# Four norm and head-group paths turned through DRAM instead of on TensorE, and a new list order, in a one-core attention and feed-forward kernel

## The chip, the cores and the metric

The kernel runs on one core of one Trainium2 chip. Times are microseconds (us) of device time of one execution. Before the change the median of three runs is 845.14 us (844.97 to 845.48). The engines are called by the names of the profile: PE is TensorE, PEld its weight loads, DVE is VectorE, ACT is ScalarE, POOL is GpSimd, SP is SyncE, which here issues the DMAs.

## The reference

A pre-norm block: attention over a dilated window of eight positions, then a SwiGLU feed-forward part, each with a residual. S = 2048 tokens, D = 640, 32 heads of 20, F = 1728.

```python
def _A_ref(x, wqkv, wo):
    qkv = (x @ wqkv).reshape(B, S, 3, H, Dh).transpose(2, 0, 3, 1, 4)
    q, k, v = qkv[0], qkv[1], qkv[2]
    idx = pos[:, None] - (jnp.arange(8) * 2)[None, :]
    ...
    logits = jnp.einsum("bhsd,bhswd->bhsw", q, kg) * Dh ** -0.5
    logits = jnp.where(mask[None, None, :, :], logits, -1e9)
    o = jnp.einsum("bhsw,bhswd->bhsd", softmax(logits), vg)
    return o.transpose(0, 2, 1, 3).reshape(B, S, D) @ wo
def _B_ref(x, w_gate, w_up, w_down):
    return (silu(x @ w_gate) * (x @ w_up)) @ w_down
h = x + _A_ref(layernorm(x), wqkv, wo)
out = h + _B_ref(layernorm(h), w_gate, w_up, w_down)
```

## The kernel before

**Blocks.** The 2048 tokens are four blocks of 512 (b = 0 to 3), each held as four rows of 128 partitions (j = 0 to 3). The heads are four groups of eight (g = 0 to 3, 160 columns each). Every fp32 product on PE is made of three passes over operands split into a high part (ACT's cast) and a low part (DVE's subtraction).

**Stages of a block.** (1) The first norm of x, and its transposition into columns, which PE needs as the stationary operand. (2) QKV (L546), group by group, 15 matmuls of 480 columns for each row; ACT evicts and scales (L551), and q, k and v go to the DRAM buffers qsc, ksc, vsc. (3) Attention, on DVE: it loads q, k and v windows, multiplies (L595), reduces (L602), takes maximum and difference (L613, L614); ACT makes the exponential; DVE sums and normalises (L624 to L626), multiplies by v (L630) and halves the products down (L638). The output is turned by 32 x 32 blocks (STREAM_TRANSPOSE, L668) and stored to the DRAM buffer osc, from where it comes back in columns. (4) The output projection, called wo(b): columns from osc are split (L783, or L711 in the blocks named in TURNED), and PE runs eight pieces of 15 matmuls of 320 columns (L793); the row of x is added (L799, L804). (5) The second norm of the sum, transposed into columns again. (6) The feed-forward part in 14 tiles of 128 columns: gate and up (L863), the gate on DVE (L898, L909), down (L874). For the last two blocks this stage works on pairs of column combinations, which save matmuls (L958, L980, their operands from column_combinations). (7) A transposition back (L1160) and the final addition.

**Three ways into columns.** On PE, four transposes of 128 x 128 into one PSUM bank, then a cast and a subtraction out of it (L507 for block 0's first norm, L439 in `to_columns`, L404 in `pair_columns`, L733 in `last_columns`). Through DRAM, a whole block: `turn_rows` turns 128 x 2560 on DVE by 32 x 32 blocks (L412) and stores it in four DMAs to ysc (L414), `turned_back` loads it (L420), and `turned_columns` casts and subtracts from SBUF (L428, L429). Through DRAM, the first half of a block: `turn_pair` (L381, buffer zsc) and `pair_columns` (L395, L396), which leaves PE ten transposes for the other half.

**Which block goes which way** is said by four tuples. TURN names blocks whose second norm goes through DRAM wholly, HALF those of which the first half does, TURN1 those whose first norm does. TURNED is the other way round: blocks whose last head group is transposed on PE (`last_columns`, L733) instead of going through osc.

**Order.** All operations are collected in a `Plan`, each with its engine, an assumed cost, its dependencies by memory ranges and a priority from the table PR. `order()` starts them greedily by priority, sorts by the start found plus an entry of SHIFT, and every engine then runs its operations in that fixed order. An operation that has to wait holds up everything behind it on its engine; SP's DMAs too are issued in this order.

**Weights.** QKV weights come in 20 pieces through a staging buffer of eight slots (L519); each is cast by ACT (L520) and split by DVE (L522). The output weights use the same staging (L685, split at L688), so their load waits until the pieces that lie there are split. Feed-forward weights are split in block 0 (L857), the low parts stored to lsc and loaded again later.

## Time and profile before

| what | us |
|---|---|
| median of three runs | 845.14 (844.97 to 845.48) |
| the profiled execution | 845.0 |
| its span, first to last instruction | 843.0 |
| ACT busy | 406.5 |
| DVE: L595, L602, L630, 32 each of about 2.8 us | 270.4 |
| DMA engines, share of the span | 65.7% |

The span is what the profile records; 2.0 us of the execution's time lie outside it. Matmuls are pipelined: the time given for one is from its start to its modelled end, while the next has started already, so what a matmul costs PE is the distance between starts. In the timeline, a row with a count (x10) is a run of equal operations, with the start of the first and the time until the end of the last. "DVE operation b <- ACT a" in the list of waits means that DVE stood idle until ACT ended a. The DMA lines give the median time from issue to landing. The granted TensorE clock was 1.0 throughout.

### The profile page before, as it was taken

How to read it: one execution, taken by the hardware profiler on the slowest of the kernel's cores; microseconds unless marked ns; L12 is line 12 of the kernel's file. 1: busy time of each engine (PE TensorE's matmuls, PEld its weight loads, DVE VectorE, ACT ScalarE, POOL GpSimd, SP SyncE). 2: the span in 40 equal slices, each digit the busy share in tenths (PEclk: the TensorE clock that was granted, in tenths of full speed). 3: DMA queues.
4: the chain of work that ended last, by engine and by line, in shares of the span. 5: the costliest groups of instructions: out<-in, count | busy, mean ns of one | idle time of the engine just before them, and what ended most of it. 6: DMA issues, size and time to landing. Idle time of an engine off the chain costs nothing.

```text
span 843.0 us, 10782 instructions
## 1 busy us (share of the span) xinstructions
PE 837.8 (99%) x3961; PEld 712.0 (84%) x3961; DVE 705.1 (84%) x841; ACT 406.5 (48%) x674; POOL 24.8 (3%) x33
## 2 busy tenths in 40 slices
PE   9999999999999999999999999999999999999998
PEld 7888888889888888888888898888888888888886
DVE  8899899999998999999999999899434996655552
ACT  6662462344663433775434467456447543333331
POOL 0000000000000100010000010000000000000000
PEclk9999999999999999999999999999999999999999
DMA  8886487467488779468987975888833554444432
GB/s 288 327 314 237 145 272 268 137 209 236 153 290 304 242 257 332 164 207 279 338 329 242 342 242 165 262 329 286 307 111 104 193 177 157 154 169 144 154 113 89
DMA packets 90260, 191.12 MB, mean 227 GB/s; under 512 B 31568, under 2 KB 50896, under 8 KB 89568
## 3 DMA queue, kind: packets, MB, share of 16 engines
q1 hardware_dynamic: 90208, 190.44, 65.7%
q8 instruction: 31, 0.51, 0.2%
q14 instruction: 21, 0.17, 0.1%
HBM read 144.26 MB, written 46.14 MB: 226 GB/s over the span
## 4 chain that ended last, share of the span: by engine, by line
PE 99%; ACT 0%; POOL 0%; DVE 0%; issue 0%; POOLq 0%
PE bank L546 25%; PE bank L874 22%; PE bank L863 22%; PE bank L958 18%; PE bank L793 8%; PE bank L980 2%; PE bank L439 1%; PE bank L454 1%; PE bank L507 0%; PE bank L404 0%; PE bank L1160 0%; PE bank L733 0%; ACT sha L509 0%; POOL ra L1194 0%; DVE h L1168 0%
## 5 line engine op out<-in xcount | busy, mean ns | idle before, releaser
L863 PE MATMUL bank<-shb,ra 128*128 128x512 f32 x810 | 190.2, 390 | 0.0
L863 PEld LDWEIGHTS bank<-shb,ra 128*128 128x128 f32 x810 | 151.4, 188 | 31.4 <-DVE shb L443 0.3
L874 PE MATMUL bank<-ra,acts 128*128 128x512 f32 (+1 forms) x662 | 162.8, 389 | 0.0
L874 PEld LDWEIGHTS bank<-ra,acts 128*128 128x128 f32 x662 | 122.5, 188 | 24.6
L546 PE MATMUL bank<-ra,sha 128*128 128x480 f32 x480 | 105.9, 380 | 0.3 <-ACT sha L509 0.3
L546 PE MATMUL bank<-ra,shb 128*128 128x480 f32 x470 | 102.8, 378 | 0.0
L546 PEld LDWEIGHTS bank<-ra,sha 128*128 128x128 f32 x480 | 89.6, 188 | 14.1 <-ACT sha L509 0.6
L546 PEld LDWEIGHTS bank<-ra,shb 128*128 128x128 f32 x470 | 88.0, 188 | 13.2
L630 DVE TENSOR_TENSOR fa<-fa 128x2560 f32<-128x2560 f32 x32 | 90.3, 2822 | 0.8
L595 DVE TENSOR_TENSOR fa<-fa 128x2560 f32<-128x2560 f32 x32 | 90.2, 2820 | 0.4
L602 DVE TENSOR_REDUCE fa<-fa 128x128 f32<-128x2560 f32 x32 | 89.9, 2810 | 0.5
L551 ACT ACTIVATE st<-bank,fa 128x480 f32<-128x480 f32 x64 | 42.2, 661 | 95.5 <-PE bank L546 87.0
L958 PE MATMUL bank<-shb,ra 128*128 128x512 f32 x360 | 88.0, 391 | 0.0
L958 PEld LDWEIGHTS bank<-shb,ra 128*128 128x128 f32 x360 | 67.1, 188 | 13.5
L638 DVE TENSOR_TENSOR fa<-fa 128x1280 f32<-128x1280 f32 (+2 forms) x68 | 75.9, 1115 | 1.5
L1096 DVE TENSOR_TENSOR fa<-bank,fa 128x512 f32<-128x512 f32 x60 | 41.0, 690 | 42.1 <-PE bank L958 41.1
L793 PE MATMUL bank<-ra 128*128 128x320 f32 x480 | 74.6, 309 | 0.0
L793 PEld LDWEIGHTS bank<-ra 128*128 128x128 f32 x480 | 72.3, 188 | 2.2 <-DVE ra L711 0.2
L958 PE MATMUL bank<-ra 128*128 128x512 f32 x288 | 68.4, 390 | 0.0
L958 PEld LDWEIGHTS bank<-ra 128*128 128x128 f32 x288 | 53.9, 188 | 11.7 <-ACT shb L1017 0.4
L840 ACT CAST ra<-fa 128x1280 fp32r<-128x1280 f32 (+1 forms) x38 | 45.9, 1207 | 28.2 <-PE bank L863 21.4
L908 ACT CAST acts<-fa 128x512 fp32r<-128x512 f32 x47 | 29.1, 620 | 50.7 <-DVE fa L898 25.5
(152 smaller groups left out, 843.7 us busy)
## 6 DMA issues: line engine op xcount, KB each, us to landing
fa<-in_ffn_dram SPq DMA_DIRECT2D x46, 960.0 KB, 6.6
ra<-lsc SPq DMA_DIRECT2D x45, 320.0 KB, 3.4
fa<-ksc SPq DMA_DIRECT2D x16, 880.0 KB, 5.6
fa<-vsc SPq DMA_DIRECT2D x16, 880.0 KB, 6.9
ra<-lsc SPq DMA_DIRECT2D x21, 640.0 KB, 5.3
lsc<-ra SPq DMA_DIRECT2D x13, 640.0 KB, 5.8
ksc<-st SPq DMA_DIRECT2D x16, 320.0 KB, 2.6
qsc<-st SPq DMA_DIRECT2D x16, 320.0 KB, 2.7
```

What stands on the lines that cost most here:

```text
L546: T.matmul(banks[bk][:, 0:480], l, r_(wq(g, w, c), 480), start=(p, c) == first_mm, stop=(p, c) == last_mm)
L551: P.add("ACT", act(480) + 0.06, lambda bk=bk, j=j: A.activation(stage_t()[:, so : so + 1920].rearrange("p (t j c) -> p t j c", t=3, j=NJ)[ ...
L595: P.add("DVE", dve(2560), lambda: V.tensor_tensor(f(PROD, 2560).rearrange("p (j w c) -> p j w c", j=2, w=W), window(ko, 2 * jp), f(qo + 32 ...
L602: P.add("DVE", dve(2560), lambda: V.tensor_reduce(f(lo + 128 * jp, 128), f(PROD, 2560).rearrange("p (n d) -> p n d", d=DH), axis=AX.X, op= ...
L630: V.tensor_tensor(f(PROD, 2560).rearrange("p (j w d) -> p j w d", j=2, d=DH), bass.AP(tensor=fa[:, vo : vo + 160].tensor, offset=fa[:, vo ...
L638: V.tensor_add(dst(v), v[:, :, 0:m, :], v[:, :, m : 2 * m, :])
L793: T.matmul(banks[bk][:, 0:320], l, r_(m, 320), start=p == 0 and c == 0, stop=p == 2 and c == NC - 1)
L840: P.add("ACT", act(n), lambda: A.copy(r_(gu, n), f(raw, n)), r=[rf(raw, n)], w=[rr(gu, n)], prio=PR["fh"])
L863: T.matmul(banks[bk], r_(gu + 1280 * w + wid * c + col, 128), x2(a, c), start=p == 0 and c == 0, stop=p == 2 and c == NC - 1)
L874: T.matmul(banks[bk][:, lo:hi], l, m, start=first and p == 0, stop=last and p == len(passes) - 1)
L958: T.matmul(banks[bk], r_(ws[w] + 256 * q, 128), x(a, c), start=start and p == n == q == 0, stop=stop and p == 2 and n == len(terms) - 1 an ...
L1096: dv(0, lambda: V.tensor_add(fb(h, dst), banks[bk], fb(h, src)), [pb(bk)] + fr(h, src), fr(h, dst))
```

## The change

**Sets.** TURN goes from () to (3,): block 3's second norm goes through DRAM wholly. TURNED goes from (0, 3) to (3,): block 0's last head group goes through osc. HALF gains block 0, TURN1 gains block 1; the latter's first norm takes its statistics on ACT instead of DVE. `column_combinations` now reads the result in the layout that the DRAM path leaves, in operations of 512 columns instead of 1024. PE had 136 transposes and has 78.

**Order.** `order()` no longer goes by PR alone: after a first list by priority it computes, from PE's list backwards, the latest start of each operation (`latest`), lists again by that (`listed`), and does so in seven rounds. On DVE an operation that reads the result of the one before it is put behind another. The assumed costs are adjusted, and SHIFT has 57 entries instead of 12.

```diff
-TURN = ()
-TURNED = (0, 3)
-HALF = (1, 2)
-TURN1 = (2, 3)
+TURN = (3,)
+TURNED = (3,)
+HALF = (0, 1, 2)
+TURN1 = (1, 2, 3)
...
+LANES, HOP = 8, 0.035
+LAP = {"PE": 0.0, "ACT": 0.1, "DVE": 0.08, "POOL": 0.0, "SP": 0.0}
+ROUNDS = ((1.0, 20, 1.5), (1.5, 10, 3.5), (1.1, 0, 1.5), (1.4, 20, 3.5), (1.3, 3, 2.5), (1.2, 3, 2.5), (1.3, 20, 5.0),)
...
 SHIFT = {
-    10: 0.9, 12: 2.5, 34: 4.5, 47: -27.4, 113: 0.8, 131: -5.8, 2096: 10.8, 2101: 6.1, 2156: 4.1, 2712: 6.9,
...
+    26: 0.6, 31: -47, 34: -25.1, 35: -4.3, 39: -16.4, 42: 1.8, 53: -0.6, 118: 0.9, 136: -103.6, 214: 10.2, 241:
...
     def order(self):
+        start = self.listed()
+        for stretch, serial, dma in ROUNDS:
+            start = self.listed(self.latest(start, stretch, dma), serial)
...
+    def latest(self, start, stretch, dma):
+
+        ops = self.ops
+        t, due = 5.0, {}
+        for n in sorted((n for n, o in enumerate(ops) if o[0] == "PE"), key=lambda n: start[n]):
+            due[n] = t
+            t += ops[n][1]
+        last = [0.0] * len(ops)
+        for n in reversed(range(len(ops))):
+            eng, cost, _, _, prio, _, nbytes = ops[n]
+            if eng == "SP":
+                cost += nbytes + dma
+            elif eng == "DVE" and prio == 20:
+                cost *= stretch
+            last[n] = min(min((last[m] - HOP for m in self.succ[n]), default=1e9) - cost, due.get(n, 1e9))
+        return last
...
+            if e == "DVE" and before is not None:
+                n = min(ready[e], key=lambda x: (x[0] + serial * (before in ops[x[1]][3]), x))[1]
...
             if b:
-                if b == 1:
-                    st.prio = PR["ln1d"]
-                    for j in range(NJ):
-                        st.one_dve(j)
-                else:
-                    for j in range(NJ):
-                        st.one(j)
+                for j in range(NJ):
+                    st.one(j)
                 st.prio = 2
                 st.rstd(0, NJ)
-                if b in TURN1:
-                    turn_rows(ysc, "Y", b, PR["tr"], PR["yst"])
-                    return
-                x_columns(
...
+                if b:
+                    turn_rows(ysc, "Y", b, *((PR["y1"],) * 2 if b == 1 else (PR["tr"], PR["yst"])))
                 return
...
-            if b in (1, 2) and b not in HALF:
+            if b not in HALF and (b in (1, 2) or b in TURN):
                 stats.rstd(0, NJ)
                 for j in range(NJ):
                     stats.apply(j)
+            if b in TURN:
+                turn_rows(ysc, "Y", b, PR["g1"], PR["g1"])
...
-            dv(0, lambda: V.tensor_add(tv(0), y(0), y(2)), yr)
+            dvs(0, lambda i: V.tensor_add(part(tv(0), i), y(i), y(2 + i)), yr)
...
             if b < 3:
                 x_columns(lambda u: (shb[:, 512 * u : 512 * u + 512], shb[:, 2560 + 512 * u : 3072 + 512 * u]), lambda u: (hi(u), lo(u)), prio)
                 return
+            if b in TURN:
+                turned_back(ysc, "Y", b, PR["g1"])
+                turned_columns(lambda: r_(X3, 5120), "ra", PR["g1"])
+                return
...
                 elif b == 1:
                     load_x(b)
                     ln1(b)
+                    turned_back(ysc, "Y", b, PR["y1"])
+                    turned_columns(*xt(b), PR["y1"])
```

In the changed file the lines have moved: L580 is QKV, L827 the pieces of wo, L899 gate and up, L910 down, L1016 the first use of block 3's columns; L629 the attention multiplication by q, L556 the split of a QKV weight piece, L719 the load of the output weights, L619 the load of a K or V window; L447 and L767 the transposes on PE for half blocks and for the last head group; L745 and L817 the splits of osc columns; L455 and L457 the turn through DRAM and its stores, L463 the load back, L471 and L472 cast and subtraction.

**How it moves the first loads.** SP's order in the first 40 us, before. L557 and L565 store k, v and q of the first group, L585 loads a K or V window, L581 q, L685 the output weights:

```order
L557 DMA ksc<-st 64x2x640
L565 DMA qsc<-st 128x640
L557 DMA vsc<-st 64x2x640
L468 DMA fa<-in_x_dram 128x1x2560
L585 DMA fa<-ksc 128x1x1760
L581 DMA fa<-qsc 128x320 x2
L585 DMA fa<-vsc 128x1x1760
L557 DMA ksc<-st 64x2x640
L565 DMA qsc<-st 128x640
L557 DMA vsc<-st 64x2x640
L685 DMA fa<-in_wo_dram 128x640 x5
```

The same place now (L591 and L599 store k, v and q):

```order
L591 DMA ksc<-st 64x2x640
L553 DMA fa<-in_wqkv_dram 128x480
L599 DMA qsc<-st 128x640
L591 DMA vsc<-st 64x2x640
L719 DMA fa<-in_wo_dram 128x640 x2
L619 DMA fa<-ksc 128x1x1760
L615 DMA fa<-qsc 128x320 x2
L619 DMA fa<-vsc 128x1x1760
L457 DMA ysc<-fa 32x20x128 x4
```

Two loads of the output weights have come ahead of the first K window, the load of block 2's x has gone behind it, and the four stores of block 1's turned rows follow.

**How it moves wo(0) on PE.** Before, from the first piece of wo(0) to the end of block 0's transposes for the second norm:

```order
L793 MATMUL bank_75<-ra 128x320 x15
L793 MATMUL bank_73<-ra 128x320 x15
L793 MATMUL bank_74<-ra 128x320 x15
L793 MATMUL bank_75<-ra 128x320 x15
L733 MATMUL bank_73<-fa 32x128
L733 MATMUL bank_73<-fa 128x128
...
L439 MATMUL bank_75<-fa 128x128 x4
L439 MATMUL bank_74<-fa 128x128 x4
L546 MATMUL bank_70<-ra,shb 128x480 x15
L439 MATMUL bank_73<-fa 128x128 x4
L439 MATMUL bank_75<-fa 128x128 x4
L439 MATMUL bank_74<-fa 128x128 x4
```

Now:

```order
L827 MATMUL bank_74<-ra 128x320 x15
L827 MATMUL bank_75<-ra 128x320 x15
L827 MATMUL bank_73<-ra 128x320 x15
L827 MATMUL bank_74<-ra 128x320 x15
L580 MATMUL bank_70<-ra,shb 128x480 x15
...
L447 MATMUL bank_74<-fa 128x128 x4
L447 MATMUL bank_75<-fa 128x128 x4
L447 MATMUL bank_73<-fa 128x128 x2
```

The transposes of the last head group between the halves of wo(0) are gone, and the second norm keeps ten of its twenty.

**Block 3's second norm on DVE.** Before, it had no turn there; now it stands among the gates (L934, L945) of the feed-forward part, and ends in five subtractions, with the first of the column combinations (L1060, L1065) around them:

```order
L409 TENSOR_TENSOR fa<-fa 128x4
L934 TENSOR_TENSOR fa<-bank_74,fa 128x512
L945 TENSOR_TENSOR acts<-fa,acts 128x512
L455 STREAM_TRANSPOSE fa<-fa 128x2560
L934 TENSOR_TENSOR fa<-bank_74,fa 128x512
L945 TENSOR_TENSOR acts<-fa,acts 128x512
L934 TENSOR_TENSOR fa<-bank_74,fa 128x512
L945 TENSOR_TENSOR acts<-fa,acts 128x512
L1060 TENSOR_TENSOR fa<-fa 128x4x128
L1065 TENSOR_TENSOR fa<-shb,fa 128x4x128
L472 TENSOR_TENSOR ra<-fa,ra 128x4x128 x5
```

The turn (L455) and the five subtractions (L472) are what replaces the twenty transposes on PE of block 3.

More of the change, by code (lines that the diff above doesn't have):

```diff
@@ L68, in order, with listed @@
     def order(self):
+        start = self.listed()
+        for stretch, serial, dma in ROUNDS:
+            start = self.listed(self.latest(start, stretch, dma), serial)
+        self.start, self.end = start, max(t + o[1] for t, o in zip(start, self.ops))
         ops = self.ops
         left = [len(o[3]) for o in ops]
[L71 to L74 removed]
+        key = [(t + SHIFT.get(n, 0.0), n) for n, t in enumerate(start)]
+        heap, out = [key[n] for n in range(len(ops)) if not left[n]], []
+        heapq.heapify(heap)
+        while heap:
+            n = heapq.heappop(heap)[1]
+            out.append(n)
+            for m in self.succ[n]:
+                left[m] -= 1
+                if not left[m]:
+                    heapq.heappush(heap, key[m])
+        return out
+    def latest(self, start, stretch, dma):
[13 more added lines that the diff above has]
+        return last
+    def listed(self, last=None, serial=0.0):
+        ops = self.ops
+        left = [len(o[3]) for o in ops]
+        if last is None:
+            self.succ = [[] for _ in ops]
+            for n, o in enumerate(ops):
+                for d in o[3]:
+                    self.succ[d].append(n)
+        succ = self.succ
         avail = [0.0] * len(ops)
@@ L1013, in dv, with dvs @@
                 P.add("DVE", dve(size(n)), fn, r=r, w=tr(n), prio=PR["jp"])
+            def dvs(n, fn, r):
+                for i in range(size(n) // 512):
+                    P.add("DVE", dve(512), lambda i=i: fn(i), r=r, w=tr(n), prio=PR["jp"])
             def put(n, dst, key):
```

114 lines of the change are left out of this document (52 added, 62 removed), and 5 rows, old and new, of the table SHIFT.

## The prediction

> **What bounds the kernel now.** I read the page first: busy time, slices, the chain that ended last.
>
> ```profile
> span 843.0 us, 10782 instructions
> PE 837.8 (99%) x3961; PEld 712.0 (84%) x3961; DVE 705.1 (84%) x841; ACT 406.5 (48%) x674; POOL 24.8 (3%) x33
> DVE  8899899999998999999999999899434996655552
> PE 99%; ACT 0%; POOL 0%; DVE 0%; issue 0%; POOLq 0%
> ```
>
> TensorE (PE) is busy 837.8 of 843.0 us and is 99% of the chain: what leaves PE's list shortens the kernel, unless PE must then wait. The digits of VectorE (DVE) are the second fact: 9 in nearly every slice (21 us each) until about 600 us, looser behind that. So I asked next what PE waits for.
>
> ```profile
> PE bank L454 <- POOL ra L1194: 1.3, 1, 1.3
> PE bank L546 <- ACT sha L509: 0.3, 1, 0.3
> ```
>
> Those 1.6 us, both at the start, are all of its waits. But DVE keeps up only just. Here are the starts of the output projections wo(0) and wo(1) on PE (L793), with the DVE operation that each needs (L711, L783):
>
> ```profile
> 190.55 1.62 PE L793 MATMUL bank<-ra 128*128 128x320 f32 x10
> 190.37 0.42 DVE L711 TENSOR_TENSOR ra<-bank,ra 32x256 fp32r<-32x256 f32 x1
> 327.96 2.21 PE L793 MATMUL bank<-ra 128*128 128x320 f32 x14
> 326.13 1.03 DVE L783 TENSOR_TENSOR ra<-fa,ra 128x512 fp32r<-128x512 f32 x2
> 481.89 1.33 PE L793 MATMUL bank<-ra 128*128 128x320 f32 x8
> ```
>
> At wo(0) DVE ends (190.79) no earlier than PE's start, at wo(1) 0.8 us ahead of it (327.16). So the question is not only what the removed transposes cost, but whether DVE can follow a PE that comes earlier.
>
> **Term 1: the transposes leave PE.** The groups of them that the change touches, before:
>
> ```profile
> L439 PE MATMUL bank<-fa 128*128 128x128 f32 x60 | 8.0, 272 | 0.0
> L404 PE MATMUL bank<-fa 128*128 128x128 f32 x20 | 3.2, 272 | 0.0
> L733 PE MATMUL bank<-fa 128*128 128x128 f32 x8 | 2.0, 272 | 0.0
> L733 PE MATMUL bank<-fa 128*32 128x128 f32 x8 | 2.0, 272 | 0.0
> ```
>
> That is 96 (40 more, in block 0's first norm and in the last step, stay); the order of the changed kernel has 38 of them (30 at L447, 8 at L767): 58 fewer. The 272 ns are from start to modelled end and overlap with neighbours; what one costs PE is the distance between starts:
>
> ```profile
> 373.15 0.62 PE L863 MATMUL bank<-shb,ra 128*128 128x512 f32 x2
> 373.60 0.85 PE L874 MATMUL bank<-acts,ra 128*128 128x512 f32 x3
> 374.29 0.60 PE L404 MATMUL bank<-fa 128*128 128x128 f32 x4
> 374.64 1.64 PE L874 MATMUL bank<-ra,acts 128*128 128x512 f32 x6
> 29.13 1.47 PE L439 MATMUL bank<-fa 128*128 128x128 f32 x12
> 30.36 1.32 PE L546 MATMUL bank<-ra,sha 128*128 128x480 f32 x5
> ```
>
> Four take 374.64 - 374.29 = 0.35 us. The six matmuls behind them take 1.64; at 0.23 from start to start (0.69 for the three at 373.60) and 0.39 for the last I expect 5 x 0.23 + 0.39 = 1.54, so 0.10 more belongs to the four: 0.45, or 0.112 each. Twelve in a row take 1.23, 0.1025 each. The bounds are 0.0875 (0.35 / 4) and 0.112; 58 of them give 5.1 to 6.5 us. I take 0.11, since most were groups of four or less among other matmuls: **-6.4 us**. The number of other matmuls, and their sizes, are unchanged.
>
> The Trainium skill ("TensorE: Matmul & The Clock Gate", Part 4: PE-mode transpose) gives about 275 ns for a transpose within a kernel; the trace agrees as to duration (272). Taken as PE's cost it would make 58 x 0.275 = 16 us, an estimate by that page; the starts above speak against it.
>
> **Term 2: DVE's list against PE's.** DVE gains work: two more 2560-wide STREAM_TRANSPOSEs, one of 1280 and two of 320. It loses work as well: block 1's first norm takes its statistics on ScalarE (ACT), wo(0) needs fewer splits of turned pieces (20 before at L711, 10 after at L745; six more at L817), and the new order puts fewer operations directly behind the one that they read (191 such neighbours before, 127 after). The last is worth something:
>
> ```profile
> 165.89 2.83 DVE L595 TENSOR_TENSOR fa<-fa 128x2560 f32<-128x2560 f32 x1
> 168.75 2.82 DVE L602 TENSOR_REDUCE fa<-fa 128x128 f32<-128x2560 f32 x1
> 171.48 0.82 DVE L688 TENSOR_TENSOR ra<-fa,ra 128x640 fp32r<-128x640 f32 x1
> L412 DVE STREAM_TRANSPOSE fa<-fa 128x2560 f32<-128x2560 f32 x2 | 5.7, 2846 | 1.2 <-ACT fa L302 1.2
> L381 DVE STREAM_TRANSPOSE fa<-fa 128x1280 f32<-128x1280 f32 x2 | 3.0, 1506 | 0.8 <-ACT fa L325 0.8
> L668 DVE STREAM_TRANSPOSE fa<-fa 128x320 f32<-128x320 f32 x28 | 12.8, 488 | 0.1
> ```
>
> A reader of the last result starts 0.03 us after its end (165.89 + 2.83 = 168.72, start 168.75); an independent one starts 0.09 before it (171.57, start 171.48). I therefore sum DVE's list in its order by the trace's durations, plus 0.035 behind a dependent neighbour and minus 0.08 behind another. The whole goes from 706 to 698 us: the added transposes (2 x 2.85 + 1.51 + 2 x 0.49 = 8.2) are more than paid for, 64 x 0.115 = 7.4 by the neighbours alone.
>
> What decides is the sum up to each operation that PE needs. Up to the last L783 or L817 of wo(2) it was 458.8 us of work and is 442.5 (durations 466.4, less 333 x 0.08, plus 78 x 0.035). PE's own list, summed at the same rates without any wait, comes to wo(2) at 455.6 instead of 481.9, as the order places wo(1) to wo(3) earlier among the feed-forward matmuls. So DVE may have lost up to 455.6 - 442.5, about 13.0 us, by then and cost nothing; before it was 481.9 - 458.8, about 23. The same sums give 19.3 at wo(0)'s first half (PE at 194.4), 14.3 at its second (212.9), 14.5 at the feed-forward start of block 0 (235.8), 13.3 at wo(1) (313.3), 14 to 15 at wo(3) (567), over 20 behind 573. Each us that DVE has lost beyond 13.0 is a us of PE.
>
> What it will have lost: nearly all of it before its first attention operation, which waits for a load of K. Before and now:
>
> ```profile
> 30.03 0.56 SPq L585 DMA_DIRECT2D fa<-ksc  x1
> 39.68 2.81 DVE L595 TENSOR_TENSOR fa<-fa 128x2560 f32<-128x2560 f32 x1
> fa<-ksc SPq DMA_DIRECT2D x16, 880.0 KB, 5.6
> 33.89 0.66 ACT L551 ACTIVATE st<-bank,fa 128x480 f32<-128x480 f32 x1 [0.77 <-PE bank L546]
> 26.65 2.06 ACT L520 CAST ra<-fa 128x480 fp32r<-128x480 f32 x4
> 36.27 3.49 DVE L522 TENSOR_TENSOR ra<-fa,ra 128x480 fp32r<-128x480 f32 x6
> ```
>
> Before, SyncE (SP) issued it at 30.03. Now two loads of the output weights stand ahead of it on SP. They fill the staging of the 17th to 19th piece of the QKV weights, so they wait for DVE's splits of these (L556), these for ACT's casts, and the casts stand behind ACT's eviction of the seventh QKV group: 33.89 less the 12 transposes (1.23) that no longer precede it, 32.7. Eviction 0.6, three casts at 0.52 and a split of 0.6 make 35.5, two issues 0.5: K is issued at 36.0 and lands 5.6 later, at about 41.5, where DVE's list has 27.2 us of work behind it. **Lost: 14.0 to 14.5.** From there to wo(2) DVE meets further waits. Those listed from the start to 190 us that fall behind the first attention are of this kind:
>
> ```profile
> DVE sha L429 <- ACT sha L428: 2.7, 2, 2.6
> DVE fa L412 <- ACT fa L302: 1.2, 2, 0.6
> DVE fa L361 <- ACT fa L367: 1.2, 2, 0.6
> ```
>
> Together 5.1, the upper bound for more of the same; zero is the lower one, since the new order puts other work between such pairs. I take 1, nearer to zero, for that reason. So 14.3 + 1 = 15.3, less 13.0: **+2.3 us**.
>
> **Parts at nothing.** Block 3's second norm now goes chain by chain: statistics, transpose on DVE (2.85), stores, load, five casts and subtractions, with nothing of it on PE.
>
> ```profile
> 633.79 2.36 PE L793 MATMUL bank<-ra 128*128 128x320 f32 x15
> L429 DVE TENSOR_TENSOR sha<-fa,sha 128x512 fp32r<-128x512 f32 x5 | 3.2, 687 | 2.7 <-ACT sha L428 2.7
> ysc<-fa SPq DMA_DIRECT2D x8, 320.0 KB, 4.9
> fa<-ysc SPq DMA_DIRECT2D x2, 1280.0 KB, 7.9
> ```
>
> That is about 5 for the row's addition, statistics and scaling, 2.85, 4.9, 7.9 and 5 x 0.69: 24 us, with the issues some 27. It is covered: wo(3) ended at 636.2 before, by PE's list it ends at 598.7 now, and the first matmul on the result comes at 642.8, so 44 us. Without that cover it would cost its excess, us by us. Block 0's turned half has 32 us (203 to 235.8) for the same steps at half size. Block 1's columns are the thin one: PE needs them at 61.5, I get them there at 59 to 60. Twenty-two more DMAs on SP delay nothing that I find except through K above.
>
> **Sum**, against the profiled execution's 845.0 (span 843.0 and 2.0 around it; the median of the runs is 845.14): 845.0 - 6.4 + 2.3 = **840.9 us**.
>
> **Rivals.** (a) *Full gain.* K lands by 40, so that the loss stays within 13: 838.6, with the low price of a transpose 839.9. For it: before, the first attention came at 39.68. Against it: the queue ahead of K.
>
> (b) *Gain eaten.* DVE loses the upper bound as well, 14.3 + 5.1 = 19.4: PE waits 6.4, 845.0. For it: in nearly every slice to 600 us DVE has a 9, and the margin at wo(2) falls from 23 to 13. The Trainium skill ("VectorE: DVE Perf Modes", The three transpose paths and the rules behind it) speaks on this side: a whole 128 x 128 transpose belongs on TensorE, as DVE turns only 32 x 32 blocks, and the DMAs must do the rest. In this trace that rest is 12.8 us of landing, which is covered. Against (b): DVE's list is 8 us shorter.
>
> (c) *Slower, by the K load.* If the splits, the weight loads or the transfers ahead delay the first attention beyond 27.2 + 13.0 + 8.2 = 48.4 us, the loss of 21.2 costs more than the 6.4 and another 1.8; at 49.5 it is 847.9. For it: the load waits for a chain ACT, DVE, SP that was not there before. Against it: 7 us later than I get, with transfers of 5 to 8 us.
>
> (d) *It does not do what it says*: the transposes filled time in which PE would have waited: 845. Against it: only 1.6 us of waits are left to fill, and the start distances show slots of their own.
>
> (e) *A transpose costs its whole duration*: 58 x 0.272 = 15.8 less the same 2.3: 831.5. The 0.35 us for four exclude it but for surprises.
>
> **How the numbers follow.** Two runs can be told apart from about 0.2%, 1.7 us: faster is below 843.4, slower above 846.8. Forecast (up to 5 us of PE waits, 839.9 to 843.4) 0.54; full gain 0.21; (e) 0.01: faster 0.76. Gain eaten and (d) 0.14: the same. Slower (c) 0.10. Range: from the full gain at the high price, 838.5 and a little less for block 1's thin place going well, 838.2, to the case between (b) and the lower price of a transpose (845.0 + 1.3, of which half), 845.6.
>
> **What would show it.** Right: 38 such transposes on PE; PE's first L827 near 194; the first attention multiplication (L629) at 41 to 42; a few us of PE waits, at L827 or the first feed-forward matmul (L899), for DVE; none at L1016, the first use of block 3's turned columns. Wrong: PE waits at L580 near 61 (block 1's columns) or at L1016; the first L629 before 40 or past 45; waits beyond 5 us in total; or an unchanged PE busy time.

## The result, and the profile after

| | before | after |
|---|---|---|
| median | 844.89 | 843.08 |
| from, to (22 executions each) | 844.61 to 846.54 | 841.39 to 846.15 |
| the profiled execution | 845.0 | 841.39 |
| ratio of after to before | | 0.998 [0.9972, 0.9987] |

The kernel is 1.81 us faster at the median, where 4.0 was forecast (844.9 to 840.9): the sign is right, the time lies in the range, and the size is off by more than half. The profiled execution happens to be the fastest of the 22; after spreads over 4.8 us, before over 1.9. Five executions among the runs below took far longer (1190.3 to 4408.5 us), in the three that were profiled with matmuls up to 2.7 times as long (1035 ns where after has 390), and the comparisons leave these five out.

The page of after, with the rows that answer to those shown of before (span; busy time; DVE's 40 slices; shares of the chain that ended last):

```profile
span 839.3 us, 10718 instructions
PE 831.4 (99%) x3903; PEld 705.0 (84%) x3903; DVE 694.7 (83%) x823; ACT 414.0 (49%) x694; POOL 23.2 (3%) x33
DVE  8599999999999999999999999996327866655552
PE 75%; DVE 15%; DMA 4%; issue 2%; ACT 2%; SPq 1%; DVEq 0%; ACTq 0%
```

PE is busy 831.4 us instead of 837.8, with 58 instructions fewer: 6.4 us, the figure of Term 1. The last digit is chance: in two further traces of the same kernel (r2 and r3 below) PE is busy 832.6 and 833.1 us with the same 3903 instructions, so the traces give 4.7 to 6.4. And the chain is no longer PE alone (99% before, 75% now). A quarter of it runs through DVE, DMAs and ACT: the work that ends last now passes through operations that PE waits for. All waits of PE in after (waited for; total, times, longest):

```profile
PE bank L497 <- POOL ra L1239: 1.3, 1, 1.3
PE bank L899 <- DVE shb L450: 1.1, 1, 1.1
PE bank L580 <- ACT sha L543: 0.6, 1, 0.6
PE bank L541 <- DVE fa L392: 0.5, 1, 0.5
PE bank L910 <- DVE acts L945: 0.4, 2, 0.2
PE bank L994 <- DVE fa L938: 0.3, 1, 0.3
```

That is 4.2 us where before had 1.6, so 2.6 more: 1.1 at L899, 0.8 in the first 8 us (L541, and L580 where before had 0.3), 0.7 at L910 and L994. The span is PE's busy time, its waits and some 3.6 us at both ends, so the account of this execution closes by itself: 843.0 - 6.4 + 2.6 = 839.2, the span is 839.3. What it does not hold is the 1.7 us by which the median execution is slower than this one.

The biggest wait, rows of after's timeline around the feed-forward start of block 0 (start, duration, operation, idle time before it):

```profile
231.13 1.39 PE L447 MATMUL bank<-fa 128*128 128x128 f32 x10
233.67 2.82 DVE L636 TENSOR_REDUCE fa<-fa 128x128 f32<-128x2560 f32 x1
236.41 0.41 DVE L450 TENSOR_TENSOR shb<-bank,shb 128x256 fp32r<-128x256 f32 x1
236.88 9.36 PE L899 MATMUL bank<-shb,ra 128*128 128x512 f32 x40 [1.09 <-DVE shb L450]
```

The ten transposes of block 0's second norm were done at 232.5. The subtraction out of them (L450) is 0.41 us long, but stands on DVE behind an attention reduction (L636) that ends at 236.5. PE starts when L450 has ended.

### The profile page after: what moved, and what is told of

Read it like the earlier page. It is cut to its first block, busy times and chain, and to the rows that moved or that the text cites. A ratio compares the mean times of both kernels' runs of the same rounds, so it can differ in the third digit from the quotient of the medians.

```text
span 839.3 us, 10718 instructions
## 1 busy us (share of the span) xinstructions
PE 831.4 (99%) x3903; PEld 705.0 (84%) x3903; DVE 694.7 (83%) x823; ACT 414.0 (49%) x694; POOL 23.2 (3%) x33
## 4 chain that ended last, share of the span: by engine, by line
PE 75%; DVE 15%; DMA 4%; issue 2%; ACT 2%; SPq 1%; DVEq 0%; ACTq 0%
PE bank L580 20%; PE bank L910 17%; PE bank L899 17%; PE bank L994 16%; PE bank L827 5%; DVE fa L629 2%; DVE fa L636 2%; DVE fa L672 2%; DVE fa L664 2%; DMA fa<-ysc 1%; DMA fa<-in_ffn_dram 1%; DMA ysc<-fa 1%; DVE fa L934 1%; DMA fa<-in_wqkv_dram 1%; DMA fa<-osc 1%
## 5 line engine op out<-in xcount | busy, mean ns | idle before, releaser
L899 PE MATMUL bank<-shb,ra 128*128 128x512 f32 x810 | 189.7, 390 | 1.1 <-DVE shb L450 1.1
L899 PEld LDWEIGHTS bank<-shb,ra 128*128 128x128 f32 x810 | 151.4, 188 | 32.4 <-DVE shb L450 1.5
L910 PE MATMUL bank<-ra,acts 128*128 128x512 f32 (+1 forms) x662 | 161.9, 389 | 0.2 <-DVE acts L945 0.2
L910 PEld LDWEIGHTS bank<-ra,acts 128*128 128x128 f32 x662 | 122.6, 188 | 25.5 <-DVE acts L945 0.5
L580 PE MATMUL bank<-ra,sha 128*128 128x480 f32 x480 | 105.1, 379 | 0.6 <-ACT sha L543 0.6
L580 PE MATMUL bank<-ra,shb 128*128 128x480 f32 x470 | 102.5, 378 | 0.0
L580 PEld LDWEIGHTS bank<-ra,sha 128*128 128x128 f32 x480 | 89.8, 188 | 14.5 <-ACT sha L543 0.9
L580 PEld LDWEIGHTS bank<-ra,shb 128*128 128x128 f32 x470 | 88.1, 188 | 13.2
L629 DVE TENSOR_TENSOR fa<-fa 128x2560 f32<-128x2560 f32 x32 | 90.1, 2816 | 0.8 <-DMA fa<-ksc 0.4
L636 DVE TENSOR_REDUCE fa<-fa 128x128 f32<-128x2560 f32 x32 | 90.0, 2814 | 0.4
L994 PE MATMUL bank<-shb,ra 128*128 128x512 f32 x360 | 86.8, 390 | 0.3 <-DVE fa L938 0.3
L994 PEld LDWEIGHTS bank<-shb,ra 128*128 128x128 f32 x360 | 67.2, 188 | 14.6 <-DVE fa L938 0.7
L827 PE MATMUL bank<-ra 128*128 128x320 f32 x480 | 75.0, 310 | 0.0
L827 PEld LDWEIGHTS bank<-ra 128*128 128x128 f32 x480 | 72.1, 188 | 2.9 <-ACT fa L830 1.3
L585 ACT ACTIVATE st<-bank,fa 128x480 f32<-128x480 f32 x64 | 41.9, 656 | 57.2 <-PE bank L580 54.4
L994 PE MATMUL bank<-ra 128*128 128x512 f32 x288 | 68.2, 389 | 0.0
L994 PEld LDWEIGHTS bank<-ra 128*128 128x128 f32 x288 | 54.1, 188 | 11.2
```

Of the source, the lines that this page charges most:

```text
L580: T.matmul(banks[bk][:, 0:480], l, r_(wq(g, w, c), 480), start=(p, c) == first_mm, stop=(p, c) == last_mm)
L585: P.add("ACT", act(480) + 0.06, lambda bk=bk, j=j: A.activation(stage_t()[:, so : so + 1920].rearrange("p (t j c) -> p t j c", t=3, j=NJ)[ ...
L629: P.add("DVE", dve(2560), lambda: V.tensor_tensor(f(PROD, 2560).rearrange("p (j w c) -> p j w c", j=2, w=W), window(ko, 2 * jp), f(qo + 32 ...
L636: P.add("DVE", dve(2560), lambda: V.tensor_reduce(f(lo + 128 * jp, 128), f(PROD, 2560).rearrange("p (n d) -> p n d", d=DH), axis=AX.X, op= ...
L827: T.matmul(banks[bk][:, 0:320], l, r_(m, 320), start=p == 0 and c == 0, stop=p == 2 and c == NC - 1)
L899: T.matmul(banks[bk], r_(gu + 1280 * w + wid * c + col, 128), x2(a, c), start=p == 0 and c == 0, stop=p == 2 and c == NC - 1)
```

## The experiments

Three questions: what differs from one execution to the next, what makes DVE late, and what belongs to the sets and what to the order.

**The changed kernel as it is, three times more.** No edit; one look each.

> The changed kernel as it is, for a second trace. The 22 executions so far lie between 841.4 and 846.2 us (before: 844.6 to 846.5), and the profiled one was among the fastest, 841.4, with 4.2 us of waits on PE, 2.6 more than before. Theory A (DVE has no reserve from wo(0) to wo(3), so every late transfer that it meets before there becomes a wait of PE): an execution of 843 to 845 shows 6 to 8 us of PE waits, all behind DVE at L899, L827 or L580, and DVE's lag at its first attention operation or right behind it is that much larger than the 11.8 us of the first trace. Rival B (PE waits for transfers itself, in the feed-forward weights): the waits are behind DMA or ACT's casts of weights, and DVE's lag is the same as in the first trace.

> The same again, for a third trace: theories as for the second. Two traces with the same waits and different times would speak against both.

> The changed kernel as it is, for one more trace, since one of the two taken was of a chip on which every matmul took 2.7 times as long. Theory as for the second trace: more time than 841.4 shows as more wait at wo(0)'s second half (L827 at 213) and at the start, with DVE's waits for the two round trips (L472 at 54 and 129) that much longer.

Measured: r1 2621.76 us, one of the five left out; r2 842.94, r3 844.22 us. PE's waits are 4.7 us in r2 and 5.1 in r3, less than the 6 to 8 that theory A expected. The span of r2 is 1.7 us longer than the first trace's, that of r3 3.0. The same places in r3 (PE at wo(0)'s second half):

```profile
212.60 0.74 PE L827 MATMUL bank<-ra 128*128 128x320 f32 x4
213.97 0.70 PE L827 MATMUL bank<-ra 128*128 128x320 f32 x3 [0.63 <-ACT ra L816]
215.21 8.04 PE L827 MATMUL bank<-ra 128*128 128x320 f32 x53 [0.54 <-DVE ra L817]
232.82 1.57 PE L447 MATMUL bank<-fa 128*128 128x128 f32 x10
26.41 0.74 ACT L343 ACTIVATE fa<-fa 128x640 f32<-128x640 f32 x1 [3.19 <-DMA fa<-in_x_dram]
207.84 0.68 DVE L817 TENSOR_TENSOR ra<-fa,ra 128x512 fp32r<-128x512 f32 x1
```

And in the first trace of after, where PE ran through wo(0)'s second half without a stop (212.60, 60 matmuls in 8.96):

```profile
25.45 0.74 ACT L343 ACTIVATE fa<-fa 128x640 f32<-128x640 f32 x1 [2.23 <-DMA fa<-in_x_dram]
206.08 0.68 DVE L817 TENSOR_TENSOR ra<-fa,ra 128x512 fp32r<-128x512 f32 x1
```

In r3 PE comes to its ten transposes (L447) 232.82 - 231.13 = 1.7 us later, all of it lost at wo(0)'s second half. The two waits there are 1.17 us long; the other 0.5 stand in the 60 matmuls around them, busy 0.74 + 0.70 + 8.04 = 9.48 us instead of 8.96, at a granted clock of 1.00. So each wait here costs PE about 0.26 us more than its length. DVE is 207.84 - 206.08 = 1.76 us later there, and 1.5 of these stand in two of DVE's waits for round trips to DRAM. Here they are in r3 (DVE's list of waits up to 214 us):

```profile
DVE fa L455 <- ACT fa L345: 10.1, 1, 10.1
DVE shb L472 <- ACT shb L471: 2.1, 1, 2.1
```

In the first trace they are 9.1 and 1.6:

```profile
DVE fa L455 <- ACT fa L345: 9.1, 1, 9.1
DVE shb L472 <- ACT shb L471: 1.6, 1, 1.6
```

The first of them is the new first norm of block 1. Its x landed 0.96 us later (26.41 against 25.45), ACT's statistics and centring therefore ended later, and DVE, which stood before L455, was held that much longer. What DVE lost at 33 us PE paid at 213. So a part of the spread is that of transfers, and it reaches PE.

In r2 it is other transfers. Its x came when it did in the first trace (L343 at 25.45 in both), but DVE waits 2.3 us at L472 instead of 1.6 and is 0.93 us later at L817 (207.01). Another 0.6 of its 1.7 us arises at 662 us, at a gate (L945) that stands on DVE behind a subtraction (L1114) that waited 0.99 us for a load, 0.41 in the first trace. Why before spreads less isn't shown: it had no wide reserve everywhere, since at wo(1) DVE ended 0.8 us ahead of PE's start.

**The K load put back in front.** The two loads of the output weights go behind those of the second head group; SP's list:

```diff
-L719 DMA fa<-in_wo_dram 128x640 x2
 L619 DMA fa<-ksc 128x1x1760
 L615 DMA fa<-qsc 128x320 x2
 ...
 L591 DMA vsc<-st 64x2x640
+L719 DMA fa<-in_wo_dram 128x640 x2
 L615 DMA fa<-qsc 128x320
```

> The first two loads of the output weights moved behind the loads of the second attention group; nothing else is moved on any engine. In the profiled execution the first attention operation waited 0.4 us for the K window, which landed 9.5 us after its issue (median of all K loads 6.0). If the early transfers are what varies (A, by the K window), K lands by 36 to 37 instead of 38.9, the median falls to 841.0 to 841.8 and the spread to about 1 us. If the lag comes from elsewhere (ACT's centring of block 1, for which DVE's first large transpose waited 9.1 us; or later transfers), the median stays at 842.5 to 843.5 with the same spread.

Measured: 842.57 us (841.30 to 844.60, 7 executions), ratio 0.9978 [0.9967, 0.9989]: the same as after. The prediction's queue ahead of K is not what makes DVE late. The first trace of after says why:

```profile
26.34 1.31 SPq L719 DMA_DIRECT2D fa<-in_wo_dram  x2
29.40 0.56 SPq L619 DMA_DIRECT2D fa<-ksc  x1
33.41 2.85 DVE L455 STREAM_TRANSPOSE fa<-fa 128x2560 f32<-128x2560 f32 x1 [9.06 <-ACT fa L345]
36.18 2.89 DVE L556 TENSOR_TENSOR ra<-fa,ra 128x480 fp32r<-128x480 f32 x5
38.99 2.82 DVE L629 TENSOR_TENSOR fa<-fa 128x2560 f32<-128x2560 f32 x1
```

The two weight loads waited 0.9 us in all; K was issued at 29.40, not 36.0, and the first attention came at 38.99. What K waited for is the landing of its own store, in after and, longer, in kfirst (SP's lists of waits, 20 to 35 us):

```profile
SPq L619 <- DMA ksc<-st: 1.7, 1, 1.7
SPq L619 <- DMA ksc<-st: 3.4, 1, 3.4
```

So kfirst issued K at 29.68, no earlier with the weight loads out of its way. Nor did the first attention wait for K, which took 6.7 us to land after its issue in this trace (not the 9.5 of the expectation): it follows five splits (L556) that end at 39.07. DVE had stood idle before these, 9.06 us, for block 1's centring on ACT.

**Less work on DVE, everywhere in block 0.** The reduction of the logits sums half of the head dimension there:

```diff
-rearrange("p (n d) -> p n d", d=DH), axis=AX.X
+rearrange("p (n d) -> p n d", d=DH)[:, :, 0 : DH // 2 if b == 0 else DH], axis=AX.X
```

> In block 0 the sum over the head dimension (L636) takes only the first half of it: eight operations of 1.4 us instead of 2.8, so 11 us of DVE's work before wo(0) are left out; the order is the same. Theory A: DVE has 11 us of reserve at wo(0) to wo(2), PE's waits on DVE vanish, and the time is 838.6 to 839.4 with a spread under 1 us. Rival B: the waits have other releasers, so 842 to 843.5 and the same spread of 4 us.

Measured: 841.04 us (840.35 to 841.83, 4 executions), ratio 0.9953 [0.9936, 0.9969], DVE busy 684.1, so 10.6 us of work less, for 2 us of time; neither theory forecast that. In its trace, of the slowest of the four, DVE reaches the same place at 203.0 instead of 203.35; the work left out has turned into waits (DVE's list, to 214 us):

```profile
DVE fa L658 <- ACT fa L649: 6.1, 4, 3.7
DVE shb L472 <- ACT shb L471: 4.8, 2, 3.6
```

They were 1.6 each in after. Up to wo(0) DVE is thus bound here less by its work than by partners that come when they come; a reserve made by less work does not survive to 214 us. PE's wait of 1.1 at L899 stayed.

**Less work on DVE at one place.** The same halving in a single reduction, the one at 233.67 above:

```diff
+[:, :, 0 : DH // 2 if (b, g, jp) == (1, 2, 1) else DH]
```

> One reduction on DVE, the one at 233.7 us that stands ahead of block 0's last subtractions, takes half of its elements: 1.4 us less, which leaves out half of a sum for eight heads of block 1. Theory D (from the last addition of wo(0) at 222 to the first gates at 251 DVE has more listed work than PE gives it time for, 1.1 us more): the wait of 1.1 us is gone and does not come back at 247 to 252, the median is 1.0 to 1.2 lower than the changed kernel's, 841.8 to 842.1. If only the place of the work counted, the wait would come back as it did when the reduction was moved, and the median would be 842.7 to 843.5.

Measured: 840.08, 840.79 and 841.87 us, ratio 0.9953 [0.9938, 0.9968]: about 2.3 us below after's median for 1.3 us of work less (10.6 / 8 reductions), more than the work explains and with three executions a weak number, but of the sign that a DVE that binds around 237 us asks for. None of the three has a trace, so where its waits went isn't shown.

**The reduction put behind the subtractions.** The same place without a change of the work; DVE's list:

```diff
 L629 TENSOR_TENSOR fa<-fa 128x2560
-L636 TENSOR_REDUCE fa<-fa 128x128
 L450 TENSOR_TENSOR shb<-bank_73,shb 128x256
 ...
 L439 TENSOR_TENSOR shb<-fa,shb 128x2x128
+L636 TENSOR_REDUCE fa<-fa 128x128
```

> One operation moved on DVE: the reduction L636 (2.82 us) that stands between the last casts of block 0's second norm and their subtractions (L450, L439) goes behind these six. In all traces so far PE waits there for the same 1.1 us (before L899 at 237), also where 11 us of DVE's work were left out. Theory C (the lost time is a sum of separate waits, each made by what stands ahead of one gate in DVE's order, not one lag that is carried through): the 1.1 us vanish and the median falls by 1.1, to 841.7 to 842.2. Theory A (one lag, of which the largest excess counts): the wait comes back at wo(1) at 313 or wo(2) at 455, and the median stays at 842.6 to 843.3.

Measured: 843.81 us (842.82 to 845.81, 10 executions), ratio 0.9991 [0.9982, 1.0]: no gain, if anything a loss. Its trace (PE and DVE, 235 to 253 us):

```profile
236.65 10.44 PE L899 MATMUL bank<-shb,ra 128*128 128x512 f32 x45
247.57 3.70 PE L899 MATMUL bank<-shb,ra 128*128 128x512 f32 x15 [0.48 <-DVE fa L934]
252.36 0.73 PE L910 MATMUL bank<-acts,ra 128*128 128x512 f32 x2 [0.87 <-DVE acts L945]
235.83 0.42 DVE L450 TENSOR_TENSOR shb<-bank,shb 128x256 fp32r<-128x256 f32 x1 [1.14 <-PE bank L580]
```

The wait at 237 is gone and comes back at 247 and 252, 1.35 us in all, and PE's waits add up to the same 4.2 us as in the first trace of after: the reduction is only late for the next gate. And L450 could not start earlier here, since it writes columns of `shb` that PE's last QKV group still reads: DVE stood idle for PE, 1.14 us. PE thus waits for DVE at one end and holds it at the other. This order is no better there; others at this place weren't tried.

**Four places moved.** late3 puts block 3's L471 and L472, at which DVE waited at 128 us, 12 us later; f4 puts one L817 of wo(0) ahead; best does both and moves one L745 and one L1114 behind the gate operations that PE waits for (L938 at 567, L945 at 660 us); all is best with the move of fix1. The piece of best on DVE for late3 and f4:

```diff
-L472 TENSOR_TENSOR shb<-fa,shb 128x4x128
 L672 TENSOR_TENSOR fa<-fa 128x2x2x160
-L472 TENSOR_TENSOR shb<-fa,shb 128x4x128
 L664 TENSOR_TENSOR fa<-fa 128x2560
 ...
+L472 TENSOR_TENSOR shb<-fa,shb 128x4x128 x2
 L702 STREAM_TRANSPOSE fa<-fa 128x2x5x32
 ...
-L817 TENSOR_TENSOR ra<-fa,ra 128x512
+L817 TENSOR_TENSOR ra<-fa,ra 128x512 x2
```

> The five casts and five subtractions that make block 3's first columns (L471, L472) moved 12 us later on ACT and DVE. DVE waited for them at 128.7 us in all traces (1.6 us in the first, 3.6 with the work left out), though PE needs the columns only behind 185. If this wait for a round trip through DRAM is what sets DVE's lag at wo(0), and its scatter that of the times: wo(0)'s second half no longer waits for DVE (0 to 0.75 us in the traces so far), the median falls by 0.5 to 1.5 and the spread to 2 us. If the scatter is made elsewhere, the median falls by less than 0.4 and the spread stays near 4 us.

> Only the wo(0) split L817 of 512 columns moved ahead of a wait for the exponential (206.7 instead of 212.7). If this split is what wo(0)'s second half waits for in the slow executions, the median falls to 841.5 to 842.5 and nothing over 843.5 is seen; if it is the smaller split behind it, or ACT's cast for it behind the round trip through osc, the median and the spread stay as in the changed kernel (843.1; 841.4 to 846.2).

> The two moves above, and three of the same kind: the wo(0) split L817 of 512 columns ahead of a wait for the exponential; a split L745 behind a gate product (L938) at 567; a subtraction L1114 that waits for a transfer behind the gate's split L945 at 660. Theory C: each of the waits of PE behind the first matmul becomes small; 839.5 to 840.8. Theory A: no better than the best of the two single moves, 841.5 to 842.5.

> The five moves of before without the first (the reduction ahead of block 0's subtractions stays where it was, since the wait came back at 247 to 252 and cost 0.7 us more). What is left of PE's waits should be the 1.1 us at 237 and about 1 us in the rest: 840.8 to 841.6, with a spread under 1 us, as wo(0)'s second half no longer waits. If the scatter of the first of the two moves alone (841.1 to 844.3) stays, the second one did not take it away, and chance made the five equal runs of before.

> The four moves again: 840.7 to 841.7, with a spread of 1 us and at least 1.3 us below the changed kernel's 843.1, as in its first four undisturbed executions.

| kernel | executions | us, median (from, to) | ratio |
|---|---|---|---|
| after | 22 | 843.08 (841.39, 846.15) | 0.998 [0.9972, 0.9987] |
| late3 | 6 | 841.74 (841.12, 844.29) | 0.9971 [0.9959, 0.9984] |
| f4 | 10 | 842.96 (842.38, 846.86) | 0.9983 [0.9973, 0.9992] |
| all | 5 | 842.00 (841.87, 842.21) | 0.9965 [0.9953, 0.9978] |
| best | 4 | 841.25 (840.72, 841.70) | 0.9957 [0.9943, 0.997] |
| best again | 6 | 842.64 (840.51, 843.40) | 0.9967 [0.9955, 0.9979] |

The ten executions of best have a median of 841.63 us: 3.3 us faster than before, some 1.4 faster than after. The second set missed what was expected of it (840.7 to 841.7): its ratio overlaps after's, and its spread is 2.9 us. PE's waits in best's first trace:

```profile
PE bank L899 <- DVE shb L450: 0.9, 1, 0.9
PE bank L910 <- DVE acts L945: 0.2, 1, 0.2
```

With the 1.3 at the start that is 2.4 us instead of 4.2; the one at L899 remains. f4 alone does nothing: its trace still waits 0.5 for the cast (L816) ahead of that split. late3 has two executions of six at 844: the spread stays. all, with every move, is no better than late3 alone.

**best with the single reduction halved.** The edit of light2 in best.

> The four moves (those of the run best) and the one reduction at 233.7 us with half of its elements (half of a sum for eight heads of block 1 left out). If the wait at 237 is DVE's work in front of it: 1.0 lower than the four moves alone, 840.0 to 840.5. If the subtractions wait there for PE's last QKV group, which reads the columns that they overwrite, most of the 1.1 us stays: 840.8 to 841.5.

Measured: 839.75, 840.15 and 840.86 us, ratio 0.9944 [0.9929, 0.9959]: about 1.5 below best's median, about the work left out (1.3). That fits a DVE whose list sets the time around 237 us in best too; three executions, beside two sets of best that lie 1.4 us apart, don't show it by themselves.

**What 58 transposes cost.** The changed kernel with 58 of its 78 transposes issued twice (at L447, L767 and L1201; the edit of the first):

```diff
-for q in range(n):
+for q in [*range(n)] * 2:
```

> Every transpose on PE at L447, L767 and L1201 issued twice into the same place: 30 + 8 + 20 = 58 more, nothing else changed. The price taken for one was 0.11 us: 58 x 0.11 = 6.4, so 849.5 (848.2 to 850). If a transpose cost its whole 0.27 us, 858.8. If transposes were hidden in waits that PE has anyway, no more than 845.

Measured: 847.16 us (846.51 to 849.24, 5 executions), ratio 1.003 [1.0018, 1.0042].

```profile
PE 839.0 (99%) x3961; PEld 711.5 (84%) x3961; DVE 695.3 (82%) x823; ACT 414.1 (49%) x694; POOL 23.1 (3%) x33
```

PE's busy time against after's traces (831.4, 832.6 in r2, 833.1 in r3) is 5.9 to 7.6 us more, 0.10 to 0.13 a transpose, as Term 1 has it (0.11); not 0.272. The time rises by 4.1 at the median, less than the 6.4 expected: the wait at L899 is gone from its list, since a PE that comes later meets a DVE that is ready.

**Sets and order apart, without the table.** Four kernels with SHIFT emptied: the sets of before or of after under the order of before or of after.

```diff
-SHIFT = {
-    26: 0.6, 31: -47, 34: -25.1, 35: -4.3, 39: -16.4, 42: 1.8, 53: -0.6, 118: 0.9, 136: -103.6, 214: 10.2, 241:
...
+SHIFT = {}
```

> The kernel before, with its sets (136 transposes on PE), under the new order without its hand table. PE's work is that of before (837.8 us busy, 845.0 with 1.6 us of waits). If the waits of the changed kernel come from the new order, which brings wo(1) to wo(3) earlier, they show here too: 847 to 850. If they come from the sets' round trips, this kernel is at 844.5 to 846.

> The changed kernel's sets (78 transposes on PE) under the old order without a hand table: 838.6 and PE's waits. If the sets could have been had without the new order, 841 to 844. If the old order places the round trips so that DVE or PE wait for them (it does not know when a result is due), 848 or more, and the new order is what makes the sets usable.

> The changed kernel with its table SHIFT emptied: new sets, new order by latest times, none of its 57 moves by hand. Four corners are wanted, all without the table: this one, before's sets under the new order (867.4 us), the new sets under the old order (907.9), and before without its own table. Theory (the sets and the new order belong together, and what is left of the order's errors the table mends): PE meets waits of some 5 to 25 us, so 848 to 868 us. Rival T (the new order alone does it, the table is polish): at most 846. Rival U (without the table the new order is no better than the old one): 890 or more.

> The kernel before with its table of 12 entries emptied: before's sets, old order. Theory: 12 entries place single operations, the old order was made for these sets, so 845 to 855 us. Rival V (the old order without its table is no better for these sets than for the new ones): 870 or more, up to the 907.9 us of the new sets under the old order; then that 907.9 says nothing about the sets.

| median, us | before's sets | after's sets |
|---|---|---|
| order of before, no table | 847.48 (847.27, 847.80) | 907.87 (907.74, 908.32) |
| order of after, no table | 867.38 (865.91, 870.33) | 861.48 (860.07, 861.53) |
| with its own table and order | 844.89 | 843.08 |

Under the order of before the sets cost 60.4 us; under the new order they gain 5.9. PE's waits with the sets under the order of before (in that file L541 is QKV, L432 the cast of the columns that come back from DRAM):

```profile
PE bank L541 <- ACT shb L432: 32.7, 2, 20.4
PE bank L408 <- ACT fa L381: 7.1, 1, 7.1
PE bank L860 <- ACT shb L399: 5.3, 1, 5.3
```

Of 52 us more waits than in after, 32.7 are QKV waiting for columns that come through DRAM too late. With the sets of after and no table the new order is 14.0 us slower than before's own pair (861.48 against 847.48). The 57 moves by hand are worth 861.48 - 843.08 = 18.4 us, the 12 of before 2.6. So with these sets the gain needs the order, which brings the turned columns in time (that wait is gone from PE's list in the kernel without its table), and the table, which takes out the rest of the waits. That it needs the sets too is argued: before's sets under the new order had no table made for them, but PE waited only 1.6 us in before, and an order alone can win little more than that.

## Why the prediction was right and where it was wrong

**Term 1 was right, its last digit by luck.** Forecast -6.4 between bounds of 5.1 and 6.5, measured -6.4 in PE's busy time of the profiled execution, -5.2 in r2 and -4.7 in r3, where PE's waits add to its busy time; 38 transposes are left at L447 and L767. The doubled transposes bound it from the other side, 0.10 to 0.13 each. With that, rivals (d), that the transposes filled waits, and (e), that each costs its 0.272, are out.

**Term 2 is the step that failed, in its size.** "Each us that DVE has lost beyond 13.0 is a us of PE" gave +2.3. Measured against the same 845.0 - 6.4 it is 2.8 in the profiled execution and 4.5 at the median (843.08 - 838.6). Three things were wrong in it.

First its place. I took one margin, the smallest, at wo(2). There after has no wait: PE starts wo(2) at 457.35, where my list without waits had 455.6, because by then PE had already stood at an earlier gate. The margin there, the feed-forward start of block 0, was in my own figures: 14.5 us. DVE had lost 15.7 by then (time less the sum of its list, at the prediction's rates), 1.2 more, and PE waits 1.1. That DVE sets PE's time at this gate, eight further traces with the same order around it show (r2, r3, kfirst, light, late3, f4, best and best again): L450 starts there from 0.24 us earlier to 1.87 later than in the first trace, and L899 on PE starts 0.47 us behind it in every one. So the rule holds there, but gate by gate and in order of time, and with the right margin for each: at wo(0)'s second half I had 14.3, DVE had lost 14.9 by its last split there (the same reckoning), and PE did not wait, since it needs this split only after seven matmuls, 1.0 us into the half (that is where it stops for L817 in r2 and r3). PE's small waits in the list above, at L541 and L580 in the first 8 us and at L910 and L994, were gates that I had not looked at. They are 1.5 of the 2.6 us; that the total came near +2.3 in the profiled execution is luck.

Second its cause. "K is issued at 36.0 and lands 5.6 later, at about 41.5" did not happen: the two loads of the output weights waited 0.9 us, K was issued at 29.40 behind its own store, the first attention came at 38.99, below the 41 to 42 that would have shown the step right and below the 40 named as a sign of its being wrong, and K's place in the queue changed nothing when it was put back. The lag at the first attention was 11.8, not 14.0 to 14.5, 9.06 of it behind ACT's centring of block 1, a wait that the term did not have. The further waits, which I took as 1, were 3.9 (15.7 - 11.8), L472 behind its cast and L658 behind ACT's L649 among them. That the total, 15.7, nearly equals my 15.3 is two errors that cancel.

Third its spread. I worked out one execution and gave its time as the median's. In after DVE sets PE's time at the feed-forward start of block 0, in r2 and r3 at wo(0)'s second half too, so that a load of x 1 us later ends in it: in r3, 1.7 of its 3.0 us arise at wo(0)'s second half. r2, at 842.94 near the median, has 5.2 us less of busy time on PE than before and 3.1 more of waits, where -6.4 and +2.3 were forecast; the two are the 2.0 us by which it misses 840.9. A part of the busy time is itself a price of waits, as r3's 9.48 us for 8.96 show. That it is so in all executions isn't shown.

**Parts at nothing: right.** Block 1's thin place held: PE goes from block 0's columns (`sha`) into block 1's (`shb`) at 61.24 without a stop. Block 3's columns cost no wait either: the first L1016 on them follows its neighbour at 646.79. The rows of after:

```profile
57.79 3.61 PE L580 MATMUL bank<-ra,sha 128*128 128x480 f32 x16
61.24 2.97 PE L580 MATMUL bank<-ra,shb 128*128 128x480 f32 x13
644.75 2.20 PE L910 MATMUL bank<-ra,acts 128*128 128x512 f32 x9
646.79 1.30 PE L1016 MATMUL bank<-ra 128*128 128x512 f32 x5
```

Block 0's second norm does cost the 1.1 at L899, but by the part that is still transposed on PE (L450), not by the half that goes through DRAM.

**The rivals.** (a), full gain at 838.6, came within 3 us in the fastest executions; its condition, K by 40, was met, its consequence not, as the loss went on growing behind it. (b), gain eaten at 845.0, is the time at the slow end of the spread (two of 22 executions above 845, four more from 844.2 to 844.8); the slowest with a trace is r3, at 844.22. (c) had a cause that did not exist, and its price was too low as well: it counted a wait of PE at its length (below).

**Left open.** An earlier load of block 1's x, which should take out the part of the wait that varies with it, wasn't tried. How the 18.4 us of the table divide over its 57 entries wasn't either, nor a table made for before's sets under the new order.

## What to carry to other kernels

When work leaves the engine that bounds a kernel, write down, for each place where that engine waits for the next one, when it comes and when it is served, in order of time, and add up the waits as they occur, each at somewhat more than its length; the smallest margin alone finds neither the place nor the sum. Look as well at what the serving engine waits for in its turn, round trips and buffers still being read, since work taken off it can turn into those waits. Where the margin falls to nothing, forecast a spread: what a load varies by then shows in the time.

## What the hardware did that I had not expected

**PE's longer waits cost much more than their length.** The stretches around two of PE's waits in the kernel of after without its table (4.0 us up to 222.2, 2.4 us up to 656.9; window, length, busy time and count of PE, PEld, DVE, ACT and POOL, granted clock, DMA share, GB/s):

```profile
218.25:222.20 3.95, 0.00 (x0) 0.00 (x0) 1.64 (x6) 3.86 (x9) 0.00 (x0) 0.85 0.91 288
222.20:227.00 4.80, 4.78 (x18) 4.78 (x19) 2.74 (x7) 4.77 (x7) 0.00 (x0) 0.50 0.05 10
227.00:232.00 5.00, 5.00 (x33) 5.00 (x32) 4.90 (x6) 3.65 (x7) 0.00 (x0) 0.92 0.83 249
654.50:656.90 2.40, 0.00 (x0) 0.00 (x0) 2.40 (x5) 2.40 (x6) 0.00 (x0) 1.00 0.14 51
656.90:658.90 2.00, 1.98 (x7) 1.61 (x8) 2.00 (x4) 1.36 (x3) 0.00 (x0) 0.76 0.38 141
658.90:660.90 2.00, 2.00 (x6) 1.59 (x5) 2.00 (x3) 1.27 (x2) 0.00 (x0) 0.50 0.32 121
```

Behind the first wait the clock stands at 0.50 for about 5.6 us (the 4.8, and 0.8 more by the mean of 0.92 behind them), behind the second for about 3.4 (by the means of 0.76, 0.50 and 0.89 over the three stretches of 2.0 us that follow it). Stretches at 0.50 follow this kernel's waits of 2.0 and 3.4 us too (10 to 12 and 252 to 254 us). In after, whose longest waits are 1.3 and 1.1, it is 1.00 around both; what a wait between 1.3 and 2.0 does isn't shown:

```profile
4.00:8.00 4.00, 2.92 (x14) 1.95 (x13) 3.70 (x9) 1.60 (x4) 0.00 (x0) 1.00 1.00 321
232.00:238.00 6.00, 4.91 (x25) 3.93 (x24) 5.97 (x6) 5.31 (x10) 1.72 (x2) 1.00 0.62 221
```

What that costs stands in the page of the kernel without the table:

```profile
span 859.7 us, 10725 instructions
PE 840.6 (98%) x3903; PEld 711.0 (83%) x3903; DVE 694.9 (81%) x823; ACT 415.3 (48%) x696; POOL 22.8 (3%) x33
```

PE is busy 9.2 us longer than in after (831.4) with the same 3903 instructions, nearly half of the 20.4 us by which the span is longer; the waits themselves, 15.0 us instead of 4.2, make the rest. Its mean granted clock is 0.990, that of after 0.999: about 8 us of time, an estimate from the two and the spans, so the clock is most of the 9.2. The Trainium skill ("TensorE: Matmul & The Clock Gate", Part 1: The HAM clock gate) gives an idle window of about 3.4 us behind which PE falls to half its clock; the wait of 4.0 agrees with it, those of 2.0 and 2.4 are shorter than the window.
